# Reusing the transposed score tiles of an attention stage in front of a mixture of experts

## The chip, the cores and the metric

The kernel runs on one core of one Trainium2 chip. The metric is the device time of one execution in microseconds (us), lower is better. Three runs before the change took 1522.19 to 1523.18 us, median 1522.53 us. Matrix products run on PE (TensorE; PEld is its weight load), elementwise work on DVE (VectorE) and ACT (ScalarE), scatters on POOL (GpSimd). SP (SyncE) issues almost all transfers.

## What is computed

```python
# attention: B=8 batches, S=1856 positions, z has 64 features, u and v 256
scores = (1.0 / S) * np.matmul(z, z.transpose(0, 2, 1))     # symmetric
attn = np.maximum(scores, 0.0) ** 2
x = (u * np.matmul(attn, v)).reshape(B * S, 256)
# experts: the best of 4 groups by x @ w_group, the best of 4 experts in it
# by x @ w_expert[g], weight = product of the two softmax values
h = np.maximum(x_e @ w1[g, e], 0.0)      # 256 -> 1024
out[tokens] = weight[:, None] * (h @ w2[g, e])   # 1024 -> 256
```

The score matrix of a batch is z times its own transpose, so it equals its transpose, and so does `attn`.

## The kernel before

**Precision.** PE multiplies in fp32r. Wherever more is wanted, an operand is split into a rounded high part (`ah`, `vh`, `z2h`, `xh`) and the rest (`al`, `vl`, `z2l`, `xl`): ACT or DVE writes the high part, DVE subtracts for the low one, and PE adds three products.

**Attention.** The work of a batch is cut into four query chunks c of 512, 512, 416 and 416 columns (`QW`, `QO`) and, for each, 15 key tiles k of 128 rows (the last has 64). A step s is one (b, c, k); there are 480. `scores(s)` (L290) does two matmuls into a bank of `ps_s` (three banks), ACT takes the relu and then the square into `r`, DVE rounds `r` to `ah` (L309; for k = 4 and 10, `ACT_TWICE`, ACT does that with a second square), and DVE writes `al = r - ah` (L312). `attn_v(s)` (L319) multiplies `ah` and `al` by the v tiles: six matmuls, four for the last key tile, into two accumulating banks of `ps_o`. All of a chunk's matmuls have the chunk's width as their number of columns. Scores run `LEAD` = 6 steps ahead of attn_v.

**Moving operand of the scores.** `prep_zm` (L243) gathers `zm` for the next chunk, z's high part in the upper 64 partitions and the low part in the lower 64, with two to four small DMAs from SBUF to SBUF. `prep_z` and `prep_v` load and split the next batch's z and v at the steps that the table `PREP` (L834) names.

**End of a chunk.** `chunk_end` (L342) multiplies the two accumulated banks by u (`xT`), splits xT into `xh` and `xl`, lets ACT write 16-bit planes that DMA transposes turn into token rows (`planes`), and computes the router's logits with four matmuls (`logits`). `defer(step, fn)` puts such pieces one or two steps later. After two chunks `route` runs a chain of some 25 small DVE operations, three small matmuls (`pk`) and eight scatters by POOL into the expert buckets in DRAM; `run_gens` advances it by three pieces per step.

**Experts.** After the last batch's routing has been sorted (`sort_experts`), 16 experts are worked off in blocks of up to 512 tokens: `phase1` (x to h) and `phase2_t` (h to y, 96 matmuls in all for a block), with the next expert's weights loaded and split in between. Blocks of the first two experts start while the last batch is still being routed.

**Order.** A scheduler that simulates the program decides the order of the instructions of each engine, except for those in `pin`, which keep the order of the code. Each engine then works through its own list strictly in order and waits on semaphores. Buffers come from pools with tags: `q` (27 buffers: z, ah, al), `r` (4), `vb` (18: v, expert weights and their raw form), `xh`, `xl` (2 each).

Of the kernel before, what the change touches and what calls it, by code (L numbers as in the profile page):

```python
# [29 lines left out]
def tile_glu_attn_moe(  # L30
# [38 lines left out]
    ACT_TWICE = (4, 10)  # L69
# [36 lines left out]
    def new_xhl(name):  # L106
        return (sb("xh", [P, ND, 512], F32R, 2, f"xh_{name}"), sb("xl", [P, ND, 512], F32R, 2, f"xl_{name}"))
# [58 lines left out]
    def load_w(e, wt, piece, name):  # L166
# [116 lines left out]

    steps = [(b, c, k) for b in range(B) for c in range(NQ) for k in range(NK)]
# [5 lines left out]
    def scores(s):  # L290
        b, c, k = steps[s]
        w = QW[c]
# [7 lines left out]
        a = sb("r", [P, 512], F32, 4, f"r_{s}")[:, 0:w]  # L300
# [3 lines left out]
        if k in ACT_TWICE and s >= NK:  # L304
# [30 lines left out]
    def load_ut(b, c):  # L335
        w = QW[c]
        t = sb("ut", [P, ND, 512], F32, 2, f"ut_{b}_{c}")[:, :, 0:w]
        held = pin if b == 0 or (b, c) == (1, 0) else same
        held(nc.sync.dma_start(t, uT[b, :, QO[c]:QO[c] + w].rearrange("(d p) q -> p d q", p=P)))
        ut[(b, c)] = t  # L340

    def chunk_end(s):  # L342
        b, c, k = steps[s]
        w = QW[c]
# [796 lines left out]
```

## Time and profile before

| | before |
|---|---|
| three runs, us | 1522.19, 1522.53, 1523.18 |
| profiled execution, us | 1518.89 |
| its span (first to last instruction), us | 1517.2 |
| mean granted clock of TensorE | 0.997 |
| PE busy | 1501.6 us, 99% |
| DVE busy | 1083.6 us, 71% |
| ACT busy | 994.3 us, 66% |
| one of the batches 2 to 6, us | 101.88 |
| attention ends, experts begin (us in the span) | about 832 |

The profiled execution's span is 1.7 us below its time; the median of the runs is 3.6 us above it. A busy PE is one with a matmul anywhere in its pipe, so the busy share alone does not say how densely matmuls are issued: the distance of their starts does. Durations of single instructions on DVE and ACT include some overlap with the next one, so a sum of durations is above the busy time that the windows give.

### The profile page before, as it was taken

To read this page: it belongs to the slowest core of one execution; us is meant where nothing else is said; L and a number is where in the kernel's file an instruction comes from. 1 tells how busy PE (TensorE), PEld (TensorE's weight loads), DVE (VectorE), ACT (ScalarE), POOL (GpSimd) and SP (SyncE) were. 2 spreads that over 40 slices of the span, in tenths; PEclk is the share of its full clock that TensorE was granted. 3 is DMA by queue.
4 is the path that set the end of the run, shared out by engine and by line. 5 is a ranking of instruction groups with operands and counts; after the bars stand their busy time and mean duration, and the time that the engine had idled before them with its cause. 6 is when DMAs were issued, how large, how long until landed. Compare 5 with 4: busy or idle time off the path is not lost. (4 is left out here: it accounts for less than half of the span.)

```text
span 1517.2 us, 22949 instructions
## 1 busy us (share of the span) xinstructions
PE 1501.6 (99%) x7449; PEld 1328.7 (88%) x7449; DVE 1083.6 (71%) x2329; ACT 994.3 (66%) x1836; POOL 288.1 (19%) x365
## 2 busy tenths in 40 slices
PE   8999999999999999999999999999999999999997
PEld 7898898988988989889889799998888888999986
DVE  6678778778786887787878658577666566666664
ACT  7888888887888888878787445444444444444442
POOL 0002221122102201221122221211221122222112
PEclk9999999999999999999999999999999999999999
DMA  9994333343334433533252564644544455445521
GB/s 291 322 255 128 102 110 93 96 117 97 102 88 116 106 92 84 128 88 97 67 143 58 143 153 112 141 119 119 120 119 113 113 135 134 133 129 131 127 57 43
DMA packets 325034, 186.48 MB, mean 123 GB/s; under 512 B 244751, under 2 KB 304147, under 8 KB 324912
## 3 DMA queue, kind: packets, MB, share of 16 engines
q1 hardware_dynamic: 312864, 153.96, 40.3%
q0 software_dynamic: 11968, 30.90, 6.1%
q8 instruction: 59, 0.97, 0.3%
q14 instruction: 63, 0.52, 0.1%
q10 hardware_dynamic: 80, 0.13, 0.0%
HBM read 72.50 MB, written 53.43 MB: 83 GB/s over the span
## 5 line engine op out<-in xcount | busy, mean ns | idle before, releaser
L312 DVE TENSOR_TENSOR al<-r,ah 128x512 fp32r<-128x512 f32 (+1 forms) x448 | 286.7, 640 | 105.5 <-ACT r L306 86.9
L330 PE MATMUL o<-ah,vl 128*128 128x416 f32 (+1 forms) x960 | 355.7, 371 | 1.5 <-DVE vl L277 1.5
L331 PE MATMUL o<-ah,vh 128*128 128x416 f32 (+1 forms) x960 | 354.7, 370 | 0.0
L302 ACT ACTIVATE r<-sc 128x512 f32<-128x512 f32 (+1 forms) x480 | 259.2, 554 | 110.4 <-PE sc L299 101.3
L333 PE MATMUL o<-al,vh 128*128 128x512 f32 (+1 forms) x896 | 288.8, 370 | 0.0
L765 PE MATMUL yT<-hh,w_e 128*128 128x512 f32 (+12 forms) x1120 | 268.7, 360 | 0.9 <-ACT hh L697 0.9
L703 DVE SCALAR_TENSOR_TENSOR hl<-ph,hh 128x512 fp32r<-128x512 f32 (+12 forms) x288 | 172.4, 609 | 135.5 <-ACT hh L697 135.1
L697 ACT ACTIVATE hh<-ph 128x512 fp32r<-128x512 f32 (+12 forms) x288 | 153.1, 536 | 142.7 <-PE ph L694 141.3
L308 ACT ACTIVATE r<-r 128x512 f32<-128x512 f32 (+1 forms) x418 | 241.6, 592 | 4.8
L543 POOL DMA_INDIRECT bucket<-rows,di x128 | 134.6, 1052 | 478.9 <-DVE di L520 231.9
L765 PEld LDWEIGHTS yT<-hh,w_e 128*128 128x128 f32 x1120 | 200.2, 188 | 26.0 <-ACT hh L697 1.3
L790 POOL DMA_INDIRECT out_dram<-y,meta x126 | 126.5, 1004 | 496.2 <-DVE y L788 476.1
L693 PE MATMUL ph<-xh_m,w1h_e 128*128 128x512 f32 (+12 forms) x576 | 206.3, 358 | 0.0
L692 PE MATMUL ph<-xh_m,w1l_e 128*128 128x512 f32 (+12 forms) x576 | 206.0, 359 | 0.0
L694 PE MATMUL ph<-xl_m,w1h_e 128*128 128x512 f32 (+12 forms) x576 | 201.9, 359 | 0.0
L330 PEld LDWEIGHTS o<-ah,vl 128*128 128x128 f32 x960 | 180.6, 188 | 22.8 <-DVE vl L277 2.1
L331 PEld LDWEIGHTS o<-ah,vh 128*128 128x128 f32 x960 | 180.5, 188 | 18.8
L309 DVE CAST ah<-r 128x512 fp32r<-128x512 f32 (+1 forms) x418 | 166.4, 400 | 42.1 <-ACT r L308 40.7
L333 PEld LDWEIGHTS o<-al,vh 128*128 128x128 f32 x896 | 168.4, 188 | 20.0
L298 PE MATMUL sc<-zm,z2h 128*128 128x512 f32 (+1 forms) x480 | 179.7, 374 | 3.4 <-DMA zm<-z2l 2.3
L299 PE MATMUL sc<-zm,z2l 128*128 128x512 f32 (+1 forms) x480 | 178.3, 372 | 0.0
L765 PE MATMUL yT<-hl,w_e 128*128 128x512 f32 (+12 forms) x560 | 158.8, 360 | 0.0
(159 smaller groups left out, 1740.1 us busy)
## 6 DMA issues: line engine op xcount, KB each, us to landing
raw_e<-in_w_dram SPq DMA_DIRECT2D x64, 512.0 KB, 5.3
bucket<-padrow SPq DMA_DIRECT2D x32, 660.0 KB, 8.5
vr<-in_v_dram SPq DMA_DIRECT2D x24, 512.0 KB, 4.2
ut<-in_uT_dram SPq DMA_DIRECT2D x16, 512.0 KB, 4.1
ut<-in_uT_dram SPq DMA_DIRECT2D x16, 416.0 KB, 3.3
zr<-in_zT_dram SPq DMA_DIRECT2D x47, 128.0 KB, 3.8
out_dram<-y,meta POOLq DMA_INDIRECT x129, 2.6
vr<-in_v_dram SPq DMA_DIRECT2D x8, 256.0 KB, 2.9
```

The lines of the kernel that those rows point to most:

```text
L298: held(nc.tensor.matmul(ps[:, 0:w], z2h[:, ks], zm, start=True, stop=False))
L299: held(nc.tensor.matmul(ps[:, 0:w], z2l[:, ks], zm, start=False, stop=True))
L302: held(nc.scalar.activation(out=a, in_=ps[:, 0:w], func=AF.Relu, scale=1.0 / S))
L308: held(nc.scalar.activation(out=a, in_=a, func=AF.Square))
L312: held(nc.vector.tensor_sub(out=al, in0=a, in1=f32(ah)))
L330: held(nc.tensor.matmul(o, vl[:, dsl], ah, start=(k == 0), stop=False))
L331: held(nc.tensor.matmul(o, vh[:, dsl], ah, start=False, stop=(k == NK - 1)))
L333: held(nc.tensor.matmul(o, vh[:, dsl], al, start=False, stop=False))
L692: nc.tensor.matmul(o, wt["l"][d][:, fs], xh[:, d, 0:W], start=(d == 0), stop=False)
L693: nc.tensor.matmul(o, wt["h"][d][:, fs], xh[:, d, 0:W], start=False, stop=False)
L694: nc.tensor.matmul(o, wt["h"][d][:, fs], xl[:, d, 0:W], start=False, stop=(d == ND - 1))
L765: nc.tensor.matmul(o, wt["2"][f // 2][:, w0:w0 + P], hs[f][q // 2][:, 0:n], start=((f, q) == (0, 0)), stop=((f, q) == (NF - 1, 2)))
```

## The change

- **Chunks.** In batches 1 to 7 the queries are cut at 512, 1024 and 1536 (blocks 0, 1, 2 of 512 and block 3 of 320) and taken in the order block 0, 3, 1, 2 (`INNER`). Batch 0 keeps the old widths.
- **Mirrored tiles.** Between two of the blocks 0, 1 and 2 the score tile of (queries i, keys j) is the transpose of that of (queries j, keys i). The chunk that comes first computes it and also stores it: DVE transposes `r` in squares of 32 (`mt`, a STREAM_TRANSPOSE), and SP writes it to a DRAM tile `sym` (256 KB each). The later chunk computes no scores for these key tiles: SP reads `at` back in four DMAs of 256 KB for four key tiles, in runs of 512 bytes, ACT casts a quarter of it to `ah`, DVE subtracts to get `al`. Block 0 stores 8 tiles, block 1 stores 4; block 1 reads 4, block 2 reads 8. That is 12 tiles in each of seven batches. `load_mirror` is called five score steps ahead (`ATL`).
- **Order.** From step 15 to the last chunk, PE, ACT and DVE keep the order of the code (`manual_schedule`). DMAs and POOL are still scheduled.
- **Later chunk ends.** xh moves to step +2, xl to +3, planes to +3 and +4, logits to +7, their copy to +8, the routing to +15; `route` now says how many steps to pause (9 before the `pk` matmuls).
- **Buffers and small things.** `r` and `mt` come from `q` (31 buffers); xh and xl come from `vb`; the high part of w1 has a tag of its own, shared with `at`. In batch 0 `zm` is copied by DVE and not by DMA. Which steps use ACT twice depends on the chunk. The loads of z, v and of the first expert's weights stand at other steps.

PE, where the third chunk of a middle batch goes over into its fourth (`o` accumulates attention times v, `sc` are scores, the number behind it is the step, counted over all batches). Before:

```order
L298 MATMUL sc_285_6084<-zm_4_3_6056,z2h_4_0_4885 128x416
L299 MATMUL sc_285_6084<-zm_4_3_6056,z2l_4_0_4886 128x416
L333 MATMUL o_4_2_0_5912<-al_280_5994,vh_4_2_4461 128x416
L333 MATMUL o_4_2_1_5913<-al_280_5994,vh_4_2_4461 128x416
L298 MATMUL sc_286_6105<-zm_4_3_6056,z2h_4_0_4885 128x416
L299 MATMUL sc_286_6105<-zm_4_3_6056,z2l_4_0_4886 128x416
```

And of the change, from the last scores of that chunk (step 284) on:

```order
L355 MATMUL sc_284_5990<-zm_4_2_5616,z2h_4_3_5112 128x512
L356 MATMUL sc_284_5990<-zm_4_2_5616,z2l_4_3_5113 128x512
L390 MATMUL o_4_2_0_5788<-ah_278_5831,vl_4_2_4900 128x512
L391 MATMUL o_4_2_0_5788<-ah_278_5831,vh_4_2_4899 128x512
L393 MATMUL o_4_2_0_5788<-al_278_5834,vh_4_2_4899 128x512
L390 MATMUL o_4_2_1_5789<-ah_278_5831,vl_4_2_4900 128x512
L391 MATMUL o_4_2_1_5789<-ah_278_5831,vh_4_2_4899 128x512
L393 MATMUL o_4_2_1_5789<-al_278_5834,vh_4_2_4899 128x512
L390 MATMUL o_4_2_0_5788<-ah_279_5860,vl_4_2_4900 128x512
```

Two score matmuls stood between the six of each step; for the eight steps 285 to 292 they are gone, and PE goes from one step's six to the next.

ACT at the same place (relu L302 or L359, square L308 or L366; `z2h` and `vh` are high parts for the next batch). Before:

```order
L302 ACTIVATE r_285_6087<-sc_285_6084 128x416
L308 ACTIVATE r_285_6087<-r_285_6087 128x416
L302 ACTIVATE r_286_6108<-sc_286_6105 128x416
L308 ACTIVATE r_286_6108<-r_286_6108 128x416
L302 ACTIVATE r_287_6127<-sc_287_6124 128x416
```

Of the change:

```order
L344 CAST ah_287_6029<-at_4_0_2_5885 128x512
L242 CAST z2h_5_0_6039<-zr_5_0_5882 128x512
L344 CAST ah_288_6043<-at_4_0_2_5885 128x512
L344 CAST ah_289_6056<-at_4_1_2_5985 128x512
L344 CAST ah_290_6066<-at_4_1_2_5985 128x512
L344 CAST ah_291_6090<-at_4_1_2_5985 128x512
L344 CAST ah_292_6109<-at_4_1_2_5985 128x512
L418 CAST xh_4_2_6119<-xT_4_2_6074 128x512 x2
L293 CAST vh_5_2_6127<-vr_5_2_5983 128x1024
L359 ACTIVATE r_293_6134<-sc_293_6131 128x512
```

The casts from `at` took the places of relu and square. The first that reads `at_4_1_2` (step 289) waits for that load, and behind it on ACT stand three casts, the chunk's xh, a v split and the relu of step 293.

DVE in the first chunk of the same batch, before:

```order
L309 CAST ah_248_5334<-r_248_5332 128x512
L312 TENSOR_TENSOR al_248_5337<-r_248_5332,ah_248_5334 128x512
L309 CAST ah_249_5352<-r_249_5350 128x512
L312 TENSOR_TENSOR al_249_5355<-r_249_5350,ah_249_5352 128x512
L312 TENSOR_TENSOR al_250_5371<-r_250_5366,ah_250_5368 128x512
```

Of the change:

```order
L370 TENSOR_TENSOR al_248_5238<-r_248_5233,ah_248_5235 128x512
L310 STREAM_TRANSPOSE mt_4_0_8_5240<-r_248_5233 128x4x4x32
L423 TENSOR_TENSOR xl_3_3_5224<-xT_3_3_5169,xh_3_3_5223 128x512 x2
L606 TENSOR_REDUCE sm_3_0_0_5253<-y_3_0_0_4955 128x40
L608 TENSOR_SCALAR sm_3_0_0_5253<-sm_3_0_0_5253 128x40
L367 CAST ah_249_5263<-r_249_5261 128x512
L370 TENSOR_TENSOR al_249_5266<-r_249_5261,ah_249_5263 128x512
L310 STREAM_TRANSPOSE mt_4_0_9_5268<-r_249_5261 128x4x4x32
```

A transpose follows each `al` of a stored tile, and the late pieces of the chunk end (`xl`) and of the routing (`sm`) stand between the steps where the code has them.

SP, where the last mirrored load of that batch is issued, after the change (it has no counterpart before):

```order
L318 DMA sym_4_2_2_5838<-mt_4_2_10_5900 128x512
L318 DMA sym_4_2_2_5838<-mt_4_2_11_5929 128x512
L326 DMA at_4_1_2_5985<-sym_4_2_2_5838 32x16x128
L476 DMA_TRANSPOSE lgx_4_0_5492<-lgp_4_1_5768 128x6x48
L326 DMA at_4_1_2_5985<-sym_4_2_2_5838 32x16x128 x3
```

The four loads stand right behind the last two of the four stores that they need. In the last batch the transposing load of the first expert's rows (`xp_0`) stands between the second and third of the stores, where SP also waits for eight scatters:

```order
L318 DMA sym_7_2_2_9573<-mt_7_2_9_9601 128x512
L453 DMA_TRANSPOSE rows_7_1_9456<-pl_7_1_9458 128x4x128
L738 ISA
L738 DMA_TRANSPOSE xp_0_9587<-bucket_69 128x4x512
L741 ISA
L741 DMA meta_0_9589<-bucket_69 128x4x2
L318 DMA sym_7_2_2_9573<-mt_7_2_10_9630 128x512
L318 DMA sym_7_2_2_9573<-mt_7_2_11_9652 128x512
```

The last two stores, and with them the loads of the last chunk's second half, are so behind the routing of the batch before.

The diff, cut to its core (the step tables and the renamed widths are left out):

```diff
-    QW = [512, 512, 416, 416]
-    QO = [0, 512, 1024, 1440]
+    MB = (1, B)
+    EDGE = [512, 512, 416, 416], [0, 512, 1024, 1440]
+    INNER = [512, S - 1536, 512, 512], [0, 1536, 512, 1024]
+    QW, QO = ([(INNER if MB[0] <= b < MB[1] else EDGE)[i] for b in range(B)] for i in range(2))
...
-    ACT_TWICE = (4, 10)
+    ACT_TWICE = ((4, 8, 12), (6, 10), (10,), (4, 10))
+    KT = 4
+    MC = 3
+    KB = [0, 3, 1, 2]
+    POS = [KB.index(i) for i in range(NQ)]
+    ATL = 5
...
-        return (sb("xh", [P, ND, 512], F32R, 2, f"xh_{name}"), sb("xl", [P, ND, 512], F32R, 2, f"xl_{name}"))
+        return tuple(new_vb(f"{h}_{name}").rearrange("p (d q) -> p d q", d=ND) for h in ("xh", "xl"))
...
-                hi, lo = new_vb(f"w1h_{name}_{piece}"), new_vb(f"w1l_{name}_{piece}")
+                if piece == 0:
+                    wt["hh"] = new_at(f"w1h_{name}", F32R)
+                hi, lo = wt["hh"][:, piece * F:(piece + 1) * F], new_vb(f"w1l_{name}_{piece}")
...
+            if b == 0:
+                held = pin if c == 1 else same
+                held(nc.vector.tensor_copy(out=zm[0:DQ, dst], in_=f32(z2h[0:DQ, src])))
+                held(nc.vector.tensor_copy(out=zm[DQ:P, dst], in_=f32(z2l[DQ:P, src])))
+            else:
+                nc.sync.dma_start(f32(zm[0:DQ, dst]), f32(z2h[0:DQ, src]))
+                nc.sync.dma_start(f32(zm[DQ:P, dst]), f32(z2l[DQ:P, src]))
...
+    def mirrored(b, c, k):
+        return MB[0] <= b < MB[1] and KB[c] < MC and k // KT < MC and POS[k // KT] < c
+
+    def put_mirror(b, c, k, a):
+
+        t2 = new_zraw(f"mt_{b}_{c}_{k}")
+        nc.vector.transpose(
+            out=t2.rearrange("p (j t x) -> p t j x", t=KT, x=32), in_=a.rearrange("p (t j x) -> p t j x", t=KT, x=32)
+        )
+        cc, kk = k // KT, k % KT
+        pair = (b, KB[c], cc)
+        if pair not in sym:
+            sym[pair] = tc.dram_tile([KT * P, 512], F32, name=f"sym_{b}_{c}_{cc}")
+        h = P if k < NKF else TAIL
+        nc.sync.dma_start(sym[pair][kk * P:kk * P + h, :], t2[0:h])
+
+    def load_mirror(b, c, cc):
+
+        g = 512 // 32
+        at = new_at(f"at_{b}_{c}_{cc}").rearrange("p (g x) -> p g x", x=P)
+        src = sym.pop((b, c, cc))[0:g * 32, :].rearrange("(g r) (j x) -> j r g x", r=32, x=P)
+        for j in range(4):
+            nc.sync.dma_start(at[j * 32:(j + 1) * 32, 0:g, :], src[j])
+        ats[(b, c, cc)] = at[:, 0:g, :].rearrange("p g (t x) -> p t g x", t=KT)
...
+        ld = steps[min(s + ATL, NS - 1)]
+        if ld[2] % KT == 0 and mirrored(*ld):
+            load_mirror(ld[0], ld[2] // KT, KB[ld[1]])
+        if mirrored(b, c, k):
+            at = ats[(b, k // KT, KB[c])][:, k % KT]
+            ah, al = new_z(f"ah_{s}")[:, 0:w], new_z(f"al_{s}")[:, 0:w]
+            nc.scalar.copy(out=ah.rearrange("p (g x) -> p g x", x=32), in_=at)
+            nc.vector.tensor_sub(
+                out=al.rearrange("p (g x) -> p g x", x=32), in0=at, in1=f32(ah).rearrange("p (g x) -> p g x", x=32)
+            )
+            hl[s] = (ah, al)
+            return
...
-        a = sb("r", [P, 512], F32, 4, f"r_{s}")[:, 0:w]
+        a = new_zraw(f"r_{s}")[:, 0:w]
...
+        mirror = MB[0] <= b < MB[1] and KB[c] < MC and k // KT < MC and c < POS[k // KT]
+        if k in (ACT_TWICE[c] if MB[0] <= b < MB[1] else (4, 10)) and s >= NK:
...
+        if mirror:
+            put_mirror(b, c, k, a)
...
+        LG = (7 if b == B - 1 else 7) if s + 1 < NS - NK else 2
+        XO = 2 if s + 1 < NS - NK else 0
+        (split_x() if XO == 0 else defer(s + XO, split_x))
+        (rest_x() if XO == 0 else defer(s + XO + 1, rest_x))
+        defer(s + XO + 1, lambda: planes(0))
+        defer(s + XO + 2, lambda: planes(1))
+        defer(s + LG, logits)
+        defer(s + LG + (1 if XO else 0), logits_out)
+        wait = 5 if last else 12 if b == 0 and c < 2 else 15 if s + 1 < NS - NK else 8
...
-        for _ in range({(B - 1, 1, 0): 24, (B - 1, 1, 1): 14}.get((b, half, hs[0]), 6)):
-            yield
+        yield {(B - 1, 1, 0): 5, (B - 1, 1, 1): 2}.get((b, half, hs[0]), 9)
...
+        if s == NK:
+            region.enter_context(tc.manual_schedule(engines={mybir.EngineType.PE, mybir.EngineType.Activation, mybir.EngineType.DVE}))
+        if s == NS - NK:
+            region.close()
```

## Rows read from the trace of the kernel before

**Rows 1.** Part 1 of the page: busy us, share, instructions by engine.
```profile
PE 1501.6 (99%) x7449; PEld 1328.7 (88%) x7449; DVE 1083.6 (71%) x2329; ACT 994.3 (66%) x1836; POOL 288.1 (19%) x365
```

**Rows 2.** Window of a middle batch: length, busy us by engine.
```profile
core 0: us, PE busy (x) PEld busy (x) DVE busy (x) ACT busy (x) POOL busy (x), PEclk, DMA share, GB/s
229.37:331.25 101.88, 101.88 (x496) 90.18 (x495) 79.28 (x189) 84.91 (x164) 18.70 (x24) 1.00 0.38 102
```

**Rows 3.** Waits of PE, whole span: us, times, longest.
```profile
PE sc L298 <- DMA zm<-z2l: 2.3, 1, 2.3
PE o L330 <- DVE vl L277: 1.5, 1, 1.5
PE warm_ps L818 <- POOL ones L119: 1.3, 1, 1.3
PE sc L298 <- ACT r L302: 1.0, 1, 1.0
PE yT L765 <- ACT hh L697: 0.9, 1, 0.9
```

**Rows 4.** Timeline of PE: first matmuls of expert blocks.
```profile
980.85 0.39 PE L692 MATMUL ph<-xh_m,w1l_e 128*128 128x512 f32 x1
1002.64 0.28 PE L692 MATMUL ph<-xh_m,w1l_e 128*128 128x256 f32 x1
...
1302.48 0.35 PE L692 MATMUL ph<-xh_m,w1l_e 128*128 128x416 f32 x1
1320.41 0.39 PE L692 MATMUL ph<-xh_m,w1l_e 128*128 128x512 f32 x1
...
891.25 0.31 PE L692 MATMUL ph<-xh_m,w1l_e 128*128 128x320 f32 x1
905.32 0.28 PE L692 MATMUL ph<-xh_m,w1l_e 128*128 128x256 f32 x1
```

**Rows 5.** DVE groups by shape, five batches: busy us, mean ns.
```profile
L312 DVE TENSOR_TENSOR al<-r,ah 128x512 fp32r<-128x512 f32 x140 | 96.6, 690 | 24.6 <-ACT r L306 20.0
L312 DVE TENSOR_TENSOR al<-r,ah 128x416 fp32r<-128x416 f32 x140 | 82.5, 589 | 49.4 <-ACT r L306 44.4
L309 DVE CAST ah<-r 128x512 fp32r<-128x512 f32 x131 | 54.8, 421 | 10.7 <-ACT r L308 10.2
L309 DVE CAST ah<-r 128x416 fp32r<-128x416 f32 x130 | 49.0, 377 | 11.3 <-ACT r L308 11.0
L277 DVE TENSOR_TENSOR vl<-vr,vh 128x1024 fp32r<-128x1024 f32 x15 | 18.3, 1221 | 1.2 <-ACT vh L276 0.7 <-DMA vr<-in_v_dram 0.5
```

**Rows 6.** ACT groups by shape, the same stretch.
```profile
L302 ACT ACTIVATE r<-sc 128x512 f32<-128x512 f32 x150 | 86.0, 595 | 35.0 <-PE sc L299 32.5 <-DVE al L312 1.0
L308 ACT ACTIVATE r<-r 128x512 f32<-128x512 f32 x130 | 79.5, 634 | 1.3
L230 ACT CAST z2h<-zr 128x512 fp32r<-128x512 f32 x15 | 9.2, 611 | 0.0
```

**Rows 7.** DMA issues: count, KB, median us to landing.
```profile
raw_e<-in_w_dram SPq DMA_DIRECT2D x64, 512.0 KB, 5.3
...
vr<-in_v_dram SPq DMA_DIRECT2D x8, 256.0 KB, 2.9
...
bucket<-rows,di POOLq DMA_INDIRECT x128, 2.7
```

**Rows 8.** Timeline of SP, last batch: start, us on its queue.
```profile
771.75 1.19 SPq L399 DMA_TRANSPOSE lgx<-lgp  x1
777.85 0.59 SPq L250 DMA_DIRECT2D zm<-z2h  x1
782.19 4.26 SPq L657 DMA_TRANSPOSE xp<-bucket  x1
```

**Rows 9.** Timeline of POOL: first and last of eight scatters.
```profile
766.38 1.28 POOL L543 DMA_INDIRECT bucket<-rows,di  x1 [38.29 <-DVE skey L561]
776.08 0.86 POOL L543 DMA_INDIRECT bucket<-rows,di  x1 [0.30 <-issue]
```

More of the change, by code (lines that the diff above doesn't have):

```diff
@@ L53, in tile_glu_attn_moe @@
     NQ = 4
-    QW = [512, 512, 416, 416]
-    QO = [0, 512, 1024, 1440]
+    MB = (1, B)
+    EDGE = [512, 512, 416, 416], [0, 512, 1024, 1440]
+    INNER = [512, S - 1536, 512, 512], [0, 1536, 512, 1024]
+    QW, QO = ([(INNER if MB[0] <= b < MB[1] else EDGE)[i] for b in range(B)] for i in range(2))
     ZW = [512, 512, 512, S - 1536]
-    assert sum(QW) == S
+    assert all(sum(x) == S for x in QW)
     assert all(cv % 16 == 0 and cv >= 2 * P for cv in caps)
@@ L349, in chunk_end, with split_x, rest_x @@
         xT = sb("xT", [P, ND, 512], F32, 1, f"xT_{b}_{c}")[:, :, 0:w]
-        xh, xl = new_xhl(f"{b}_{c}")
+        xhl = []
         for d in range(ND):
             nc.vector.tensor_mul(out=xT[:, d, :], in0=oa[d][:, 0:w], in1=u_t[:, d, :])
-            nc.scalar.copy(out=xh[:, d, 0:w], in_=xT[:, d, :])
-            nc.vector.tensor_sub(out=xl[:, d, 0:w], in0=xT[:, d, :], in1=f32(xh[:, d, 0:w]))
+        def split_x():
+            xhl.extend(new_xhl(f"{b}_{c}"))
+            xh, xl = xhl
+            for d in range(ND):
+                nc.scalar.copy(out=xh[:, d, 0:w], in_=xT[:, d, :])
+        def rest_x():
+            xh, xl = xhl
+            for d in range(ND):
+                nc.vector.tensor_sub(out=xl[:, d, 0:w], in0=xT[:, d, :], in1=f32(xh[:, d, 0:w]))
         rows = new_rows(f"rows_{b}_{c}")
         nc.gpsimd.iota(rows[:, 0:nt, D + 1:RW], pattern=[[P, nt], [0, RW - D - 1]],
-                       base=b * S + QO[c], channel_multiplier=1)
+                       base=b * S + QO[b][c], channel_multiplier=1)
         part = w % P
@@ L401, in logits @@
             )
-        defer(s + 1, lambda: planes(0))
-        defer(s + 2, lambda: planes(1))
-        defer(s + 2, logits)
-        wait = 5 if last else 12 if b == 0 and c < 2 else 8
+        LG = (7 if b == B - 1 else 7) if s + 1 < NS - NK else 2
[7 more added lines that the diff above has]
+        wait = 5 if last else 12 if b == 0 and c < 2 else 15 if s + 1 < NS - NK else 8
         alone = b == B - 1 and c >= NQ - 2
@@ L422, in run_gens @@
             try:
-                next(gens[0][1])
+                gap = next(gens[0][1])
                 n -= 1
+                if gap and step < 10 ** 9:
+                    gens[0] = (step + gap, gens[0][1])
             except StopIteration:
```

84 lines of the change are left out of this document (47 added, 37 removed).

## The prediction

> **What bounds the kernel now.** I read the engine totals first. PE has a matmul in its pipe for 99% of the span, DVE works for 71%, ACT for 66% [rows 1]. A share over the whole span says little about a stage, so I then cut it into batches: in a middle batch, 101.88 us long, PE is busy for all 101.88, at full granted clock, while DVE has 79.3 and ACT 84.9 [rows 2]. The waits of PE confirm it: all the waits in 1517 us come to 7.0 us in five places, none of them repeated from batch to batch [rows 3]. So in attention the two helpers run some 20 us per batch ahead of need, and the time of a batch is the number of matmuls times the distance of their starts.
>
> That distance has to be known for each width, since the change brings in chunks of 320 columns. A busy PE doesn't give it, the expert blocks do, which have 96 matmuls of one width each: a 512 block lasts from 980.85 to 1002.64, 21.79/96 = 0.2270 us a matmul; a 416 block 17.93/96 = 0.1868; a 320 block 14.07/96 = 0.1466 [rows 4]. The steps from width to width are 0.0402 for each 96 columns, so a matmul costs its columns plus a fixed 0.0126 us, also at 320: no floor from the weight load shows down there. Check: a batch has 118 matmuls per chunk and four for the logits, 2 x 122 x (0.2270 + 0.1868) = 101.0 us, plus six small `pk` matmuls, against 101.88 measured.
>
> The Trainium skill (TensorE: Matmul & The Clock Gate, section "Back-to-back issue gap") gives an isolated gap of N/2.4 + 2.5 ns, 216 ns for 512 columns, and about 131 ns in a sustained stream. The trace has 227 and decides; by the page's figures the 168 matmuls below would be worth 36.3 or 22.0 us and not 38.1.
>
> **What leaves PE.** 12 of a batch's 60 score tiles are mirrored, each of them two matmuls of 512 columns: 24 x 7 = 168 matmuls. 168 x 0.2270 = 38.1 us, or 5.45 per batch. All 38.1 lie on the path that sets the end, since PE has no idle time there to take it up. The new widths alone change nothing: 0.2270 + 0.1466 = 0.3736, and two at 416 cost 2 x 0.1868 = 0.3736. A batch should come to 101.88 - 5.45 = 96.4 us.
>
> **What is late next: ACT.** It loses 12 relus and squares, 12 x (0.595 + 0.634) = 14.7 us, and gets 12 casts from `at`, for which the nearest row is z2h's cast of the same size, 0.611: 7.3 us [rows 6]. With a slightly shorter list of second squares its 84.9 falls to about 77, 80% of 96.4. The relu in scores stays 6 steps ahead of attn_v, 7 us even at 320 columns, which covers the late pieces of a chunk end (xh, planes, logits copy), now spread over seven steps.
>
> **DVE.** Its casts to `ah` fall from 52 to 41: before 26 x 0.421 + 26 x 0.377 = 20.8 us, now 28 x 0.421 + 13 x 0.333 (the slope between the two widths taken on to 320) = 16.1. Subtractions stay at 60 with the same number of columns. New are 12 transposes of 128x512 at an unknown price T, which no row shows. From below it's a cast, 0.421; from above I take the costliest single operation of the stage, 1.221 for a subtraction of 1024 columns [rows 5]. I choose 0.69, the subtraction of the same size, as the operation that reads and writes the same f32 columns. DVE: 79.3 - 4.7 + 12 x 0.69 = 82.9 of 96.4 us; at T = 1.22, 89.2. It passes PE only from T = (96.4 - 74.6)/12 = 1.82 us. Cost: nothing, hidden under PE; if T is at its upper end, the first chunk, with 8 of the 12, has 4.3 us more work in 27 us and I'd expect up to 1 us lost per batch.
>
> **Waits and queues.** SP gets 12 stores and 12 loads per batch, at 0.59 us of its queue each [rows 8] 14 us. I followed the tightest chain, the last load of each batch (`at` for block 2 from block 1). Clock zero is the start of the scores of the last stored tile on PE. Scores 0.45, relu 0.60, square 0.63, cast 0.42, subtraction 0.69, T 0.69: 3.5 us, and 2 more for queueing on the two engines. The store of 256 KB lands 2.9 us after its issue [rows 7]: 8.4. The four loads take 3 x 0.59 on SP with a logits transpose of 1.19 between: the last one goes at 11.4. It lands after 2.9 us (256 KB) to 5.3 (the slowest 512 KB row): 14.3 to 16.7. Cast and subtraction, 1.3: 15.6 to 18.0. PE wants the result at step 4 of the last chunk: four steps of eight matmuls (7.3), six of the chunk's rest without scores (7.7), four logits matmuls (0.6), then two steps of six and two of eight (6.4): 22.0 us. So there is 4 to 6 us to spare. Queued behind the waiting cast on ACT are three more such casts, xh and the relu of step 293, whose scores PE issues at 18.3; they have time.
>
> In the last batch the chain is longer: SP issues the third and fourth store only after it has waited for eight scatters and issued the transposing load of the first expert's rows. Scatters take 776.94 - 766.38 = 10.6 us [rows 9] and 2.7 to land [rows 7], the load 4.3 on SP's queue [rows 8], then come two stores (1.2 + 2.9), a weight load, a logits transpose, the loads (0.6, 1.2, 4 x 0.59, then 2.9 to 5.3), cast and subtraction (1.3). From the routing's last DVE piece, some 5 us before clock zero, that is 24 to 27 us on my clock against 22.0: PE stalls there once. I put 2.5 us, with 0 and 8 as ends.
>
> Program order itself: the three engines now run in an order without regard to when a piece is ready. With 6 steps in hand, and ACT and DVE at 80 and 86%, single waits vanish. I put 0.3 us per batch, 2 in all, with ends of 0 and 3 per batch, as the window of ACT at 320 columns is the narrowest.
>
> In batch 0, DVE copies `zm` in place of a DMA on which PE waited 2.3 us [rows 3]; the copies (64 partitions, under two 0.42 casts) stand in a stage where DVE has room. Gain between 0 and 2.3; I take 1.5. Logits, routing and planes are the same work later; the routing's scatters still come a chunk ahead of the next use of their buffers. The expert stage has the same instructions: its xh and xl take the room that w1's high part left in `vb`. Zero.
>
> **Sum.** -38.1 - 1.5 + 2.5 + 2 = -35.1 us on the profiled execution, 1518.9, which itself stands 3.6 below the median. At the median: 1522.5 - 35.1 = 1487.
>
> **Rivals.**
> *A. The mirrored loads come late.* They read DRAM in runs of 512 bytes, 2048 per megabyte, where the rows of 3 to 5 us move longer ones; no row bounds them from above. At raw_e's rate [rows 7] a megabyte takes 2 x 5.3 = 10.6 us from the first issue, and 8.4 + 10.6 + 1.3 = 20.3 is just in time; at half that rate it's 8.4 + 21.2 + 1.3 = 30.9, 8.9 us late in each of seven batches, 62 us: 1522.5 - 35 + 62 = 1550. It decides from a load of 17.3 us on, where PE loses the 5.0 per batch that the sum gains. Against it: the DMA engines are busy for only 0.38 of a batch [rows 2]. 10%. The Trainium skill (VectorE: DVE Perf Modes, "The three transpose paths") warns that a plain DMA that transposes by strides is 19 times slower than the transposing one if the innermost stride in the destination is large. Here 512-byte runs are contiguous at both ends, the squares having been turned by DVE, so I don't think that its condition holds; no row shows such a transfer.
> *B. Program order and DVE leak.* PE loses 2 to 3 us per batch, in chunk 0 (T near 1.2) or at 320 columns: 14 to 21 us more, 1501 to 1508. For it: DVE comes to 86 to 93%, with runs of small routing pieces in between. 17%.
> *C. PE is held altogether*, DVE being the bound with T of 2 us or more, or a wait in every step: 74.6 + 12 x 2.2 = 101 us per batch, no gain, 1520. 5%.
> The forecast, 1480 to 1496: 68%.
>
> A measurement of this kernel tells about 0.2%, 3 us, from no change. Faster: 68 + 17, 0.85; same: 4 of C; slower: A and the rest of C, 0.11. For 8 in 10 the range takes the forecast's and most of B: 1480 to 1507.
>
> **What would show it.** Middle batches of 96.4 us with PE busy for all of it; 84 STREAM_TRANSPOSEs of 0.5 to 0.8 us; DVE near 83 and ACT near 77 us per batch; four `at` DMAs landing within 5 us; no PE wait on zm early; one PE wait of a few us on `al` or `ah` from `at` at the start of the last chunk. Wrong, if PE waits on ACT or DVE in each batch, above all at the fifth step of the last chunk (A) or in the first two (B), or if matmuls at 320 columns start further apart than 0.147 us.

## The result

| | median, us | lowest to highest, runs |
|---|---|---|
| before | 1522.36 | 1519.38 to 1523.18, 4 |
| after | 1499.23 | 1497.68 to 1500.73, 4 |

The ratio is 0.9851, with a 95% interval of 0.9839 to 0.9863: 1.5% faster, 23 us, where 35 were forecast. The profiled execution after has 1499.14 us (span 1497.4); against before's 1518.89 (span 1517.2) it is 19.8 shorter. So on the basis on which the sum was made, 15.3 us of 35.1 are missing. The time lies in the range (1480 to 1507), above the forecast's own 1480 to 1496. It is in the range by the room that was left for rival B, whose mechanism did not come; in so far that was luck.

### The profile page after: what moved, and what is told of

The parts are those of the page before. It is cut to its first block, busy times and chain, and to the rows that moved or that the text cites. A ratio compares the mean times of both kernels' runs of the same rounds, so it can differ in the third digit from the quotient of the medians.

```text
span 1497.4 us, 22660 instructions
## 1 busy us (share of the span) xinstructions
PE 1468.7 (98%) x7281; PEld 1265.8 (85%) x7281; DVE 1120.0 (75%) x2330; ACT 972.3 (65%) x1724; POOL 280.6 (19%) x351
## 5 line engine op out<-in xcount | busy, mean ns | idle before, releaser
L390 PE MATMUL o<-ah,vl 128*128 128x512 f32 (+2 forms) x960 | 355.4, 370 | 1.5 <-DVE vl L294 1.5
L391 PE MATMUL o<-ah,vh 128*128 128x512 f32 (+2 forms) x960 | 355.0, 370 | 0.0
L393 PE MATMUL o<-al,vh 128*128 128x512 f32 (+2 forms) x896 | 330.5, 370 | 0.0
L370 DVE TENSOR_TENSOR al<-r,ah 128x512 fp32r<-128x512 f32 (+2 forms) x364 | 229.8, 631 | 28.1 <-ACT r L364 5.9
L359 ACT ACTIVATE r<-sc 128x512 f32<-128x512 f32 (+2 forms) x396 | 213.9, 540 | 49.8 <-PE sc L356 31.2
L624 POOL DMA_INDIRECT bucket<-rows,di x121 | 130.6, 1080 | 424.8 <-issue 267.8
L366 ACT ACTIVATE r<-r 128x512 f32<-128x512 f32 (+2 forms) x341 | 199.1, 584 | 10.8
L367 DVE CAST ah<-r 128x512 fp32r<-128x512 f32 (+2 forms) x341 | 136.0, 399 | 26.6 <-ACT r L366 23.9
L849 ACT COPY yp<-yT 128x1024 uint16<-128x1024 uint16 (+2 forms) x70 | 59.4, 848 | 146.0 <-PE yT L846 102.9
L355 PE MATMUL sc<-zm,z2h 128*128 128x512 f32 (+2 forms) x396 | 147.7, 373 | 6.6 <-ACT r L359 6.6
```

The source lines that it names most:

```text
L359: held(nc.scalar.activation(out=a, in_=ps[:, 0:w], func=AF.Relu, scale=1.0 / S))
L366: held(nc.scalar.activation(out=a, in_=a, func=AF.Square))
L370: held(nc.vector.tensor_sub(out=al, in0=a, in1=f32(ah)))
L390: held(nc.tensor.matmul(o, vl[:, dsl], ah, start=(k == 0), stop=False))
L391: held(nc.tensor.matmul(o, vh[:, dsl], ah, start=False, stop=(k == NK - 1)))
L393: held(nc.tensor.matmul(o, vh[:, dsl], al, start=False, stop=False))
```

## The profile after

Part 1 of the page answers to [rows 1]:

```profile
PE 1468.7 (98%) x7281; PEld 1265.8 (85%) x7281; DVE 1120.0 (75%) x2330; ACT 972.3 (65%) x1724; POOL 280.6 (19%) x351
```

168 matmuls are gone (7449 to 7281), and PE's busy time fell by 32.9. The windows of two middle batches, the one that lost nothing and the one that lost most, answer to [rows 2]; two windows of ten us in the last batch stand behind them:

```profile
core 0: us, PE busy (x) PEld busy (x) DVE busy (x) ACT busy (x) POOL busy (x), PEclk, DMA share, GB/s
311.48:407.69 96.21, 96.21 (x471) 81.32 (x470) 83.94 (x188) 81.59 (x149) 18.44 (x22) 1.00 0.66 171
407.69:506.35 98.66, 96.87 (x471) 81.09 (x470) 84.05 (x188) 81.35 (x149) 17.51 (x22) 1.00 0.65 167
770.00:780.00 10.00, 6.29 (x28) 4.88 (x26) 0.38 (x1) 0.00 (x0) 0.00 (x0) 0.98 1.06 207
780.00:790.00 10.00, 6.71 (x24) 5.20 (x25) 9.24 (x17) 9.15 (x15) 0.00 (x0) 0.68 0.32 89
```

Batches 1 to 6 take 97.6, 97.2, 96.2, 98.7, 96.8 and 97.2 us; in most of them PE is no longer busy for all of it. Its longest waits over the span (us in total, times, longest), against [rows 3]:

```profile
PE pl L465 <- ACT xh L418: 7.0, 1, 7.0
PE sc L355 <- ACT r L359: 6.6, 7, 1.8
PE ph L773 <- ACT xh_m L757: 2.3, 1, 2.3
...
PE pl L466 <- DVE xl L423: 1.2, 2, 0.8
```

The wait on zm is gone. New are above all one wait of 7.0 us in the last batch, those of score matmuls on ACT's relu, and one of 2.3 us at the experts' block 1. Of the seven on the relu, three (3.0 us) are in batch 0 and four (0.4 to 1.8 us, 3.5 in all) in batches 1, 2, 4 and 6.

What holds ACT is seen in its own waits, here of batches 1 to 6 (142 to 727 us):

```profile
ACT ah L344 <- DMA at<-sym: 45.1, 6, 8.9
```

and in ACT's timeline of batch 4, the one that lost most, and of the last one (start, us, and in brackets the idle time ahead of a row and what ended it):

```profile
481.20 2.19 ACT L344 CAST ah<-at 128x512 fp32r<-128x512 f32 x4 [8.87 <-DMA at<-sym]
483.78 1.22 ACT L418 CAST xh<-xT 128x512 fp32r<-128x512 f32 x2 [0.40 <-DVE xT L412]
484.91 1.04 ACT L293 CAST vh<-vr 128x1024 fp32r<-128x1024 f32 x1
485.85 0.59 ACT L359 ACTIVATE r<-sc 128x512 f32<-128x512 f32 x1
...
780.04 2.18 ACT L344 CAST ah<-at 128x512 fp32r<-128x512 f32 x4 [14.74 <-DMA at<-sym]
782.62 0.62 ACT L418 CAST xh<-xT 128x512 fp32r<-128x512 f32 x1 [0.40 <-DVE xT L412]
```

ACT stands on the last mirrored load, once per batch. PE doesn't wait for that operand: it waits for a relu (in the last batch for xh) that stands behind the casts in ACT's order. The relu at 485.85 is that of step 293, whose score PE had issued at 479.11. The scores have three banks, so that of step 296 needs the bank that this relu frees:

```profile
479.11 0.39 PE L355 MATMUL sc<-zm,z2h 128*128 128x512 f32 x1
...
486.50 0.50 PE L355 MATMUL sc<-zm,z2h 128*128 128x512 f32 x1 [1.79 <-ACT r L359]
```

SP's timeline of the same batch, and of the last one:

```profile
466.26 1.15 SPq L235 DMA_DIRECT2D zr<-in_zT_dram  x2
467.50 1.03 SPq L318 DMA_DIRECT2D sym<-mt  x2
472.29 0.32 SPq L326 DMA_DIRECT2D at<-sym  x1
472.71 1.24 SPq L476 DMA_TRANSPOSE lgx<-lgp  x1
474.01 1.69 SPq L326 DMA_DIRECT2D at<-sym  x3
...
764.76 1.86 SPq L738 DMA_TRANSPOSE xp<-bucket  x1
...
767.36 0.91 SPq L318 DMA_DIRECT2D sym<-mt  x2
...
771.13 2.11 SPq L326 DMA_DIRECT2D at<-sym  x4
```

On the prediction's clock (zero: start of the scores of the last stored tile, 460.81 in batch 4, 753.48 in the last; a landing is the start of the cast that waited for it):

| | predicted | batches 1 to 6 | batch 4 | last batch |
|---|---|---|---|---|
| last tile turned by DVE | 5.5 | 6.1 | 6.1 | 9.9 |
| last load issued | 11.4 | 12.3 to 14.3 | 14.3 | 19.3 |
| last load landed | 14.3 to 16.7 | 17.8 to 20.4 | 20.4 | 26.6 |
| first operand from it ready | 15.6 to 18.0 | 19.1 to 21.7 | 21.7 | 27.9 |
| PE takes this operand | 22.0 | 22.4 | 22.4 | held |
| relu of step 293 starts | | 22.5 to 25.0 | 25.0 | held |

And the transfers (count, KB each, median us from the start of the issue to the landing, as far as the trace has landings: 16 of the stores, 20 of the loads):

```profile
sym<-mt SPq DMA_DIRECT2D x84, 256.0 KB, 2.6
at<-sym SPq DMA_DIRECT2D x84, 256.0 KB, 5.0
```

The loads of v from 117 to 800 us, before and after:

```profile
vr<-in_v_dram SPq DMA_DIRECT2D x17, 512.0 KB, 4.0
```

```profile
vr<-in_v_dram SPq DMA_DIRECT2D x18, 512.0 KB, 7.0
```

The DMA engines are busy for 0.66 of a batch in place of 0.38, and these loads take longer too; those of u of 512 KB hardly do (3.8 to 4.1). What part of the 5.0 us of `at` is due to the traffic, and what to its runs of 512 bytes, no run separates.

**Where the missing time is.** I cut both spans at the first attn_v matmuls of batch 1 and of batch 7: before 117.5, 611.1 and 788.6 us, after 116.7, 583.7 and 797.1. Of the missing 15.3 us, 0.7 are in batch 0 (-0.8 in place of -1.5), 3.5 in batches 1 to 6 (-27.4 for -30.9) and 11.1 in batch 7 and behind it (+8.5 for -2.6). The cut at batch 7 before is good to half a us, as the scheduler mixes two batches there (728.61; two matmuls of batch 7 start ahead of it). The 583.7 is the lowest of four runs in which batches 1 to 6 have the same code: f3, g1 and e1 below have 585.8, 585.0 and 587.4.

## The experiments

The runs were on several chips, on which the kernel before had medians of 1521.9 to 1527.6; so compare ratios, each to before on the same chip (after: 0.9851), or the three stretches of the profiles. The two can differ by some us: from e2 to f4 the stretches fall by 3.5 us and the ratio doesn't. Safest are runs of one letter, which were on one chip.

| kernel | median, us | ratio (95%) | batch 0 | 1 to 6 | 7 to end |
|---|---|---|---|---|---|
| e1_late_rows | 1503.43 | 0.9838 (0.9824 to 0.9851) | 116.9 | 587.4 | 797.4 |
| e2_tiles_first | 1488.12 | 0.9744 (0.9730 to 0.9757) | 116.8 | 578.1 | 791.1 |
| e3_late_cast | 1502.70 | 0.9841 (0.9827 to 0.9854) | 116.2 | 587.6 | 796.3 |
| e4_no_order | 1537.04 | 1.0064 (1.0050 to 1.0077) | 120.2 | 612.4 | 800.9 |
| f1_no_mirror | 1526.20 | 1.0026 (1.0017 to 1.0036) | 117.0 | 611.1 | 796.0 |
| f2_cast3 | 1504.32 | 0.9885 (0.9870 to 0.9900) | 116.6 | 587.7 | 797.3 |
| f3_sp_order | 1495.81 | 0.9830 (0.9816 to 0.9844) | 116.7 | 585.8 | 792.5 |
| f4_best | 1484.28 | 0.9756 (0.9743 to 0.9769) | 116.4 | 577.0 | 789.0 |
| g1_no_last | 1497.50 | 0.9804 (0.9789 to 0.9819) | 116.8 | 585.0 | 794.0 |
| g2_best | 1482.93 | 0.9710 (0.9695 to 0.9724) | 115.9 | 577.1 | 788.3 |
| g3_w1_place | 1536.09 | 1.0049 (1.0032 to 1.0066) | 116.5 | 625.5 | 792.3 |
| g4_best_no_last | 1488.91 | 0.9746 (0.9731 to 0.9761) | 115.1 | 577.1 | 794.3 |

**e1_late_rows**

```diff
-        if s == NS - NK - 12:
+        if s == NS - NK - 6:
             load_rows(0)
```

> The load of the first expert's rows (xp_0) is issued 6 steps later, behind the last mirror loads of the last batch instead of ahead of their stores. Theory T (of the 12 us that are missing, some 7 are a stall in the last batch, where two mirror stores stand behind xp_0 on SP, some 3 are the clock that falls after that stall, and the rest is 0.9 us per middle batch): the 7.0 us wait of the logits matmul on ACT's xh falls to 2 us or less, the granted clock stays at 0.97 or more from 770 to 800 us, middle batches stay at 97.2 us; 1487 to 1492 us. Rival R1 (program order itself leaks, a little in every stage): the wait moves elsewhere, 1497 to 1501. Rival R2 (the mirror loads are slow by themselves, 7 us from issue to landing under the traffic of the last batch, wherever xp_0 stands): the wait stays at 5 us or more, 1495 to 1500.

No gain, and the wait was 6.7 us; but the experiment didn't do what it says. SP isn't in the region of program order, and its own ordering put xp_0 ahead of the fourth store again. SP's timeline of e1:

```profile
770.11 0.52 SPq L318 DMA_DIRECT2D sym<-mt  x1
771.02 2.28 SPq L738 DMA_TRANSPOSE xp<-bucket  x1
773.40 0.52 SPq L318 DMA_DIRECT2D sym<-mt  x1
```

So it shows nothing on T, and f3 repeats it.

**e2_tiles_first**

```diff
+    GO = ([0, 1, 2, 3], [0, 1, 2, 3], [0, 2, 1, 3], [0, 1, 2, 3])
...
+    def tile(b, c, k):
+        return KT * GO[c][k // KT] + k % KT if MB[0] <= b < MB[1] else k
```

(scores and attn_v take `tile(b, c, k)` for their operands)

> In batches 1 to 7 the third chunk takes its key tiles in the order of groups 0, 2, 1, 3, so that the four tiles stored for the last chunk are worked off four steps (7.3 us) earlier; all else stays. T: the loads of the last chunk find their stores landed, ACT's waits on at (up to 8.9 us, once per batch) go below 2 us, PE's waits of scores on ACT's relu go, middle batches fall from 97.2 to 96.2 - 96.5 us, and the stall of the last batch goes with them: 1484 to 1489 us. R1 (program order): the waits on at go and the middle batches stay at 97 or more; only the last batch gains, 1490 to 1494. R2 (traffic): loads still take 7 us or more after issue and the middle batches stay at 97.2; 1494 to 1500.

T held. A window of one of e2's middle batches:

```profile
309.67:405.91 96.24, 96.24 (x471) 81.33 (x470) 84.01 (x189) 81.36 (x148) 17.10 (x22) 1.00 0.66 171
```

And all that its ACT still waits for `at` in batches 1 to 7:

```profile
ACT ah L351 <- DMA at<-sym: 0.8, 2, 0.5
```

PE is busy for all 96.2 us at the same DMA share, and the 7.0 us stall of the last batch is gone. The transfers are as many; the last tile that they need is turned 7.2 to 7.8 us earlier in batches 1 to 6, and the last load is issued 3.7 to 6.0 us earlier. Against e1, which ran on the same chip and in which batches 1 to 6 are those of the changed kernel, the time is 15.3 us lower. That settles the cause in the middle batches and of the stall: the lateness of the last load of each batch.

**e3_late_cast** and **f2_cast3**

```diff
+    CLEAD = 2
...
+            if c == 3 and k // KT == 1:
+                casts.append((s - CLEAD, cast))
+            else:
+                cast()
...
+        while casts and casts[0][0] <= s:
+            casts.pop(0)[1]()
```

(`cast` makes ah and al from `at`; in f2 CLEAD is 3)

> The transfers stay where they are; only ACT's casts and DVE's subtractions of the four mirrored tiles 4 to 7 of the last chunk are issued later, 2 steps ahead of their use in place of 6, so that ACT no longer stands in its order on a load that is 5 us away. T (in the middle batches the operand itself is in time, and PE loses through ACT, which is held in order, so that the relu behind the casts comes late): scores' waits on ACT's relu go, middle batches 96.2 to 96.6; in the last batch the logits matmul no longer waits for xh, PE works three more steps (4 us) and then waits some 3 us for the operand: 1488 to 1493. The rival O (the operand is late itself): PE's waits move to attn_v on ah or al with the same size, middle batches 97.2, 1497 to 1500.

> As e3_late_cast, with the casts of the last four mirrored tiles 3 steps ahead of their use in place of 2. In e3 ACT no longer waited for the load, and PE's new wait of 1.07 us on al came from DVE's own order, which had the subtraction behind xl, vl and the routing. T (the load lands in time for the operand, and what PE lost was ACT held in order): PE's waits go from the middle batches, 96.2 to 96.6 us each; in the last batch some 2 to 4 us of wait remain; ratio to before 0.980 to 0.983. Rival O (the load is too late for the operand): 97.2 or more per batch, ratio 0.984 to 0.986.

Both missed their times. PE's first waits in e3, and then ACT's in f2's batches 1 to 6:

```profile
PE o L402 <- DVE al L349: 7.1, 8, 1.5
PE o L399 <- ACT ah L348: 4.6, 3, 3.2
```

```profile
ACT ah L348 <- DMA at<-sym: 36.5, 5, 8.9
```

With two steps the wait on the relu went from PE, as T said, but one of 0.7 to 1.5 us on `al` took its place: the late subtractions now stand behind xl, vl and the routing in DVE's order. With three steps ACT is held for up to 8.9 us as before, since it has nothing else in between, and the later subtractions are late as well (up to 1.5 us). In the last batch e3's stall fell from 7.0 to 3.2 us, with 1.4 us of smaller waits behind it. T was right that in the middle batches the operand itself is in time: in the changed kernel the first one is ready 0.6 to 3.2 us before PE takes it (table above), and in f2 as long. What T left out is the price of the later places: neither of the two gained anything in batches 1 to 6 (587.6 and 587.7), and only the earlier load of e2 did.

**e4_no_order**

```diff
-        if s == NK:
-            region.enter_context(tc.manual_schedule(engines={mybir.EngineType.PE, mybir.EngineType.Activation, mybir.EngineType.DVE}))
```

> The same work without the region in which PE, ACT and DVE issue in program order: all engines are ordered by the scheduler, as in the kernel before. R1 (program order costs the missing time): middle batches below 96.6, 1487 to 1492. T (it's the mirrored loads' lateness, that no order of the three engines takes away): middle batches at 97 or more and a stall of several us in the last batch; 1496 to 1510.

Both missed: T's 1510 was far too little, and R1 falls in the other direction. Without program order the whole gain is gone, at 101.7 to 102.4 us a batch. PE's largest wait over the span (in total), and DVE's in batches 1 to 6:

```profile
PE o L390 <- DVE ah L367: 16.8, 34, 1.4
```

```profile
DVE xT L412 <- PE o L391: 52.8, 24, 2.7
```

DVE stands at each chunk's eviction (xT), four times a batch, until PE has ended the chunk, and the casts that PE needs next stand behind it. ACT waits for `at` only 3.7 us in these six batches, so here it isn't the late load that takes the gain.

**f1_no_mirror**

```diff
-    MB = (1, B)
+    MB = (B, B)
```

> The changed kernel with an empty range of mirrored batches: every batch computes all its scores and keeps the old chunks of 512, 512, 416 and 416; the program order of PE, ACT and DVE and the later chunk ends stay. Theory T (all of the gain is the 168 matmuls, as PE had no idle time before, so that order alone has nothing to give): batches of 101.5 to 102 us, the time within 3 us of the kernel before, ratio 0.998 to 1.002. Rival G (program order is a gain by itself): ratio 0.990 or below. Rival L (program order costs something in every batch that the mirrored tiles hide): ratio above 1.004.

Batches of 101.86 us, as T said, but 0.26% slower in all, just above T's bound. The loss is all in the last stretch: 796.0 for 788.6. There f1 has waits of 1.3 us on xl and 2.6 on `ah`, and the 512-wide expert blocks take longer, 22.0 us and more against 21.78 (g3), 4.2 us over the 29 blocks compared under g3.

**f3_sp_order**

```diff
+        if s == NS - 2 * NK + 4:
+            region.close()
+            region.enter_context(tc.manual_schedule(engines={mybir.EngineType.PE, mybir.EngineType.Activation, mybir.EngineType.DVE, mybir.EngineType.SP}))
...
-        if s == NS - NK - 12:
+        if s == NS - NK - 6:
```

> In e1 SP's own ordering put xp_0 ahead of the last store again. Here SP too issues in program order from the fifth step of the last batch's third chunk to its end, so that xp_0 goes behind the last mirror loads; all else as in the changed kernel. Theory X (the last batch's stall of 7 us comes mostly from xp_0's place in SP's queue): the wait of the logits matmul falls to 3 us or less and the granted clock stays up; ratio to before 0.978 to 0.981. Theory Y (it comes mostly from the transposes of the last four tiles, which DVE ends 4 us late behind the sort, and from the slow landing under other traffic; xp_0 has 2 to 3 us of it): the wait falls to 4 to 5 us; ratio 0.982 to 0.984.

Y held, with the ratio in its range and a wait just under its 4 to 5 us:

```profile
PE pl L465 <- ACT xh L418: 3.9, 1, 3.9
```

xp_0's place costs 3 us of the stall. For the rest, DVE turned the last tile at 9.9 on the clock, behind the sort of the experts (4.1 us of it, in the changed kernel from 751.6 to 755.7), and the last load still took 5.9 us; how much each has of it isn't shown.

**f4_best** and **g2_best**

```diff
-        LG = (7 if b == B - 1 else 7) if s + 1 < NS - NK else 2
+        LG = (9 if b == B - 1 else 7) if s + 1 < NS - NK else 2
...
-        wait = 5 if last else 12 if b == 0 and c < 2 else 15 if s + 1 < NS - NK else 8
+        wait = 5 if last else 15 if s + 1 < NS - NK else 8
...
-            if b == 0:
+            if (b, c) <= (1, 0):
```

(on top of e2; the last pair, zm by DVE, is in g2 alone)

> e2_tiles_first with two more steps: the last batch's logits matmuls 9 steps behind the chunk end in place of 7 (PE waited 2.4 us there for xl, which DVE had behind the sort), and in batch 0 the routing 15 steps behind the chunk end in place of 12 (DVE, in program order, stood 4.9 us on the transposed logits, the chunk's eviction came late by it, ACT's xh and a relu behind it too, and PE waited 2.2 us). T: both waits go, 3 to 5 us less than e2, ratio to before 0.971 to 0.973. Rival: the waits move to the next piece in the same order, ratio 0.974 or above.

> f4_best with the zm of batch 1's first chunk copied by DVE like those of batch 0, in place of the two transfers on which PE waited 2.2 us in f4. T: this wait goes, batches stay at 96.2 us, about 2 us less than f4; ratio to before 0.973 to 0.975. Rival: DVE's copies delay the chunk's other pieces and a wait of the same size comes on xl or r; ratio 0.9755 or above.

The wait that f4 was to remove in batch 0 is read in e2 as a chain of three engines in program order (DVE, ACT, PE):

```profile
93.67 0.54 DVE L537 COPY lgf<-lgx 128x640 uint16<-128x640 uint16 x1 [4.88 <-DMA lgx<-lgp]
...
95.47 1.08 DVE L420 TENSOR_TENSOR xT<-o,ut 128x416 f32<-128x416 f32 x2
...
96.09 1.04 ACT L426 CAST xh<-xT 128x416 fp32r<-128x416 f32 x2 [3.19 <-DVE xT L420]
...
98.33 0.63 PE L362 MATMUL sc<-zm,z2h 128*128 128x416 f32 x1 [2.17 <-ACT r L366]
```

DVE stood on a transfer for the routing, and all behind it was late. In f4 it went, and waits of 2.2 us on the zm of batch 1 and of 1.5 us on xl came: the ratio has e2's in its interval, so the rival held there. In the last batch the wait of 2.4 us on xl went, as T said. In g2 the wait on zm falls to 0.7 us. g2 is the best kernel here, 0.971 of before, below the range of its T; in its profile the stretches are 1.6, 34.0 and 0.3 us shorter than before's, 36.0 in all.

**g1_no_last** and **g4_best_no_last**

```diff
-    MB = (1, B)
+    MB = (1, B - 1)
```

> The changed kernel with mirrored tiles in batches 1 to 6 only; the last batch computes all its scores in the old chunks. Theory T (the last batch is where the gain was lost): by the rows of the changed kernel it gives back 5.45 us of matmuls and takes away the stall of 7.2 us with about 3 us of lowered clock, and the wait of 2.4 us ahead of block 1's matmuls with 1.75 us of lowered clock behind it; the kernel without mirrors had 4.4 us of other waits in its last batch, which come in: 5.45 - 10.2 - 4.2 + 4.4 = -4.5 us, ratio to before 0.981 to 0.983. Rival M (a mirrored batch is worth its 5.45 us wherever it is, and the stalls would come anyway): ratio 0.988 to 0.990.

> g2_best with mirrored tiles in batches 1 to 6 only. T: once the loads are in time, the last batch's mirrored tiles are worth 5.45 us of matmuls less what they bring on behind attention, where the last routing, sort and load of rows start no earlier by them (the wait of 2.4 us and 1.75 us of clock at block 1): without them some 1 to 4 us slower than g2, ratio to before 0.975 to 0.978. Rival (the last batch's tiles cost more than they give even then): 1 us or more faster than g2.

(g4 is g2 with this edit.) In the changed kernel the mirrored tiles of the last batch were a loss: without them 0.9804 in place of 0.9851, as T said and slightly more (the last stretch has 3.0 us less; the runs are from different chips). Once the loads are in time they're a gain, and a larger one than I expected: g4 is 6 us slower than g2 on the same chip, all of it in the last stretch. So the 5.45 us of their matmuls do arrive at the end. The price that I set behind attention is small here: g2 waits 1.2 us longer at block 1, and g4 has 2.6 us of waits on `ah` in its last chunk that g2 has not.

**g3_w1_place**

```diff
-                if piece == 0:
-                    wt["hh"] = new_at(f"w1h_{name}", F32R)
-                hi, lo = wt["hh"][:, piece * F:(piece + 1) * F], new_vb(f"w1l_{name}_{piece}")
+                hi, lo = new_vb(f"w1h_{name}_{piece}"), new_vb(f"w1l_{name}_{piece}")
```

> f1_no_mirror with one difference: w1's high part stands in two tiles of the vb pool (22 buffers in place of 18, the at pool left out), as in the kernel before, and not in one tile of the at pool. In the changed kernel a 512 block of the experts takes 21.92 us against 21.78 before, with the same 96 matmuls, and in f1 22.0 to 22.1. Theory P (the place of w1's high part makes its matmuls start 0.006 us further apart): 512 blocks back at 21.8 or less, 4 us less than f1, ratio to before 0.999 to 1.001. Rival B (it comes with the build as a whole, the place of the instructions or of other tiles): blocks at 21.9 to 22.1, ratio 1.001 to 1.004.

First matmuls of the same 512 block and of the block behind it, in PE's timeline of after and of g3:

```profile
910.31 0.39 PE L773 MATMUL ph<-xh_m,w1l_e 128*128 128x512 f32 x1
932.25 0.28 PE L773 MATMUL ph<-xh_m,w1l_e 128*128 128x256 f32 x1
```

```profile
949.33 0.39 PE L771 MATMUL ph<-xh_m,w1l_e 128*128 128x512 f32 x1
971.10 0.28 PE L771 MATMUL ph<-xh_m,w1l_e 128*128 128x256 f32 x1
```

21.94 and 21.77, where before has 21.78 in the same block (21.79 in that of [rows 4]). From this block on, the 29 blocks ahead of the last one add up to 561.18 us before, 563.80 after, 565.41 in f1 and 561.17 in g3: P holds for the blocks. But g3 also resizes a pool, and f1 and the changed kernel, with w1's high part in the same pool, differ by 1.6 us; so which tile's place it is stays open. The total does not speak for it, since g3 waits 11.6 us for ACT's relu in attention, a cause that I did not follow.

## Why the prediction was right, and where its size was off

**The matmuls: right.** 101.88 - 5.45 = 96.4 was forecast, and a batch takes 96.2 where nothing is late (e2, g2), with matmuls of 512 and 320 columns 0.227 and 0.147 apart. By the figures of the Trainium skill (TensorE: Matmul & The Clock Gate, "Back-to-back issue gap") a batch would have lost 5.2 or 3.1 us, an estimate; it lost 5.7, so the trace does not agree.

**ACT and DVE: covered, as forecast.** DVE has 84.1 us a batch for 82.9, with T = 0.70 for the 0.69 chosen; ACT 81.3 for 77, too low by 4, which costs nothing. The prediction took sums of durations off a busy time. The durations of a batch do fall by 9 us (97.7 to 88.6), near the 8 forecast, but they overlapped by 13 us before and by 7 after.

**The load chain: wrong in size, and in what waits for it.** "4 to 6 us to spare" rested on landing times of a DMA system that was busy for 0.38. The change itself brought it to 0.66. The last stores landed 3.2 to 4.1 us after their issue in place of 2.9, the last load was issued at 12.3 to 14.3 in place of 11.4 (in batch 4, 0.6 us by DVE, 1.2 in SP's queue behind two loads of z and the third store, 1.2 by the landing), and it took 5.3 to 6.6 us in place of 2.9 to 5.3. That left 0.6 to 3.2 us for the operand itself. What failed is the sentence "queued behind ... they have time": four casts, xh and vh stand ahead of the relu, 4.7 us, so it starts at 22.5 to 25.0, and PE's score of step 296, due at 23.7, takes its bank. This is rival A in a mild form; its sign, PE waiting on ACT at the start of the last chunk, showed in four of six batches. It cost 5.6 us in batches 1 to 6 (583.7 for e2's 578.1), where 1.8 were booked, and those under the "0.3 us per batch" of program order; order itself leaks nothing there (f1: 101.86, g2: 96.2).

**The last batch: the term of 2.5 us, mis-sized.** The chain was worked out to 24 to 27 us against 22.0, that is 2 to 5 late, and I took the low end. The load was issued at 19.3, took 7.3 us, and landed at 26.6, which puts the operand at 27.9; PE stands for xh, which ACT has behind all four casts, until 29.8. From start to start of its matmuls that is a stall of 7.1 us (so counted, a stall is some 0.15 us above the profile's wait). That's 4.7 more than booked; 1.5 go with the clock behind it.

**Behind attention: "Zero", wrong.** Block 1 waits for rows that pass through the last routing, sort, scatter and load. This chain starts with the end of attention, but it has become longer: from the last matmul of attention to the cast of these rows (`xh_m`) it takes 39.1 us before (832.4 to 871.5) and 42.8 after (806.8 to 849.6). In g2 it's 42.6, and in g1 and g4, whose last chunk has 416 columns as before and not 512, 38.7. Which piece of it takes the 3.7 us isn't shown. The wait is 2.4 us, and the block behind it takes 18.41 us for 16.67, most of it by the clock (16.87 in g2, where it doesn't fall). The blocks from 910.31 on, with w1's high part in its new place, cost 2.6. With the two items above, 4.7 + 1.5 + 2.4 + 1.7 + 2.6 = 12.9, less a wait of 1.1 that before had at 844 us: 11.8, where 11.1 were to be explained.

**Batch 0: -1.5, came to -0.8.** The wait on zm went, and more than the 2.3 us that the prediction took as the upper end. Behind that wait the granted clock stood at its lower level from 30.7 to 34.1 us (0.66 of full over 30 to 35 us), which costs another 1.6 us or so by the distance of the matmuls (rows of before):

```profile
30.05 0.47 PE L298 MATMUL sc<-zm,z2h 128*128 128x512 f32 x1 [2.33 <-DMA zm<-z2l]
31.75 0.63 PE L330 MATMUL o<-ah,vl 128*128 128x512 f32 x1
32.17 0.63 PE L331 MATMUL o<-ah,vh 128*128 128x512 f32 x1
```

Against it came 3.0 us of waits on ACT's relu and 0.8 on xl, where before had 1.0 on a relu [rows 3]. With the longest of them mended, g2 has -1.6.

**B and C fell:** no leak in chunks 0 or 320 of batches 1 to 6, no holding of PE.

## What to carry to other kernels

When a change trades matmuls for transfers, work out its chains with landing times at the traffic that it will cause, not at that of the trace before. An engine in program order turns a late operand into a late everything: count all that is queued behind the waiting instruction, and move the producer earlier rather than the consumer later. A new shape for the last piece of a stage also changes the chain that starts behind it: here it became 3.7 us longer, so work that chain out as well.

## What the runs showed of the hardware

- With a wait of PE the granted clock sometimes fell to its lower level, 1.2 of 2.4 GHz. Behind the 7.0 us stall (granted clock 0.68 over 780 to 790 us) the 512 matmuls start 0.43 us apart, not 0.227, until 786.3, so 1.5 us are lost (rows of after):

```profile
783.29 0.66 PE L465 MATMUL pl<-xh,whl 128*48 128x512 f32 x1 [6.99 <-ACT xh L418]
783.75 0.63 PE L355 MATMUL sc<-zm,z2h 128*128 128x512 f32 x1
784.17 0.63 PE L356 MATMUL sc<-zm,z2l 128*128 128x512 f32 x1
784.60 0.63 PE L390 MATMUL o<-ah,vl 128*128 128x512 f32 x1
```

The wait of 2.3 us at block 1 was followed by such a fall in after (0.83 in 850 to 860 us; the next block took 18.41 us) and in f4, and not in g2 and f3 (16.87). A wait of 1.8 us in f3 (at 195 us) was followed by one, a wait of 3.2 us in e3 (at 783 us) was not; so the length of the wait alone doesn't decide, and what does is open.
- The distance of matmuls went with the placement of tiles in SBUF: a 512 block takes 21.76 to 21.80 us with w1's high part in `vb` (before, g3), 21.9 in the kernels with mirrored tiles, 22.0 to 22.1 in f1, the same for each block to 0.02 us in all kernels of one placement, unless a wait or a lower clock falls into it. Which tile does it, and why, is open.
- Transfers of 256 KB in runs of 512 bytes, issued in groups of four, landed in 5.0 us (median of the 20 landings in the trace of after), against 2.6 (median of 16) for the stores of the same size.
- A transpose of 128x512 f32 by DVE in squares of 32 (STREAM_TRANSPOSE) took 0.70 us, as a subtraction of that size (0.69).
